# Attention beside a spectral filter on one core: four zero matmuls left out, and the last matmuls of seven units moved behind scores

## The chip, the core and the metric

The kernel runs on one core of a Trainium2 chip. The metric is the device time of one execution in microseconds. The kernel before took 424.93 us in the median of three runs (424.67 to 424.96).

## What is computed

From x of 2048 x 448 the kernel computes a gated sum of two results. `a` is softmax attention with 16 heads of 28 columns each, `b` is a two-dimensional real Fourier transform, a product with given complex weights, and the inverse transform. The reference, cut to that:

```python
x = A_x
g = sigmoid((x * gate_w).sum(-1, keepdims=True))

qkv = (x @ wqkv).reshape(B, S, 3, H, Dh).transpose(2, 0, 3, 1, 4)
q, k, v = qkv[0], qkv[1], qkv[2]
scores = jnp.einsum("bhqd,bhkd->bhqk", q, k) * Dh ** -0.5
o = jnp.einsum("bhqk,bhkd->bhqd", softmax(scores, axis=-1), v)
a = o.transpose(0, 2, 1, 3).reshape(B, S, D) @ wo

X = rfft2(x.astype(float32), axes=(-2, -1)) * (w_r + 1j * w_i)
b = irfft2(X, s=(S, D), axes=(-2, -1)).astype(bfloat16)

out = g * a + (1 - g) * b
```

B is 1, S is 2048, D is 448, H is 16 and Dh is 28; the inputs are bfloat16.

## The kernel before

**Blocks of scores.** The scores of a head are 2048 x 2048. They are cut into blocks of 128 keys by 512 queries. A block is one matmul that uses 32 rows of the TensorE array (`score`, L834). Four heads make a group T (0 to 3), and a group has four blocks of queries, so c runs over 16 blocks of (group, queries); each has 16 blocks of keys, i, and four heads.

**Two ways to an exponential.** Most blocks go to ScalarE: two or three of them are written to a tile in PSUM (`ps2` or `ps3`, in turn), and one exp of 1024 or 1536 columns reads the tile (`exp`, L1092). Other blocks are packed for VectorE: `away` (L1054) writes one score block to a background bank, VectorE turns it into 16-bit integers (L850), and when four are together a chain of VectorE steps makes the exponential out of them (L870, L873, L878, L882, L885, L896 and L904, or a transfer that adds, L899, in place of the last). The chain's steps wait in a list, `vq`, and are put out one by one with `fill_v` or `hurry`.

**Values.** `do_pv` (L1440) multiplies the finished exponentials with the values: four matmuls of 32 columns of the array for each block of keys (L1013), summed in the PSUM bank `psPV`.

**Units.** All other work is cut into units, which share two PSUM banks called `bg0` and `bg1` with the packed scores. A unit has phases; a phase is some matmuls (`pe`) and what empties the bank again (`ve`), with planned costs. Of those that the change names:
- `V5`, `V9` and `V15` are value projections (`v_unit`, L500): four matmuls of 336 columns (L506) into one bank, each adding the next part of the inner dimension, and one cast (L510) that takes the sum out. Unit Vt gives the values of key block t.
- `q1.3`, `k2.1`, `q3.0` and `q3.2` are projections of q or k (`qk_unit`, L554; the first digit is the group, the second the block of 512 columns): four matmuls of 512 columns (L290, in `project`) and one cast (L562).

Other units that stand beside them: parts of the transforms (L678 and L683; L699 to L721 for the column transforms, of which L746 to L758 are the second kind of inputs; L771 to L791 for the inverse), each with its bank and its eviction.

**The order.** The order of instructions on every engine is worked out while the kernel is built. `stream` (L1368) runs one iteration k for each exp: it emits exp k, then values (`do_pv`), then units (`pick` chooses one, `step` at L1240 emits its next phase), then zero matmuls, then the scores for exp k+2 (`scores`, L1016). The planner keeps a clock for each engine: `self.tp` for TensorE, `self.tv` for VectorE, `self.ta` for ScalarE. It moves them by constants written in the code, and asks by them whether a phase still fits. `self.bank_free` holds when a bank should be empty, and a new unit takes the bank that is free first. The engines themselves wait for each other's results by semaphores, in the planned order.

**Behind scores.** A phase named in the set `BEHIND` (L56) is planned at its place in the iteration, but its matmuls and its eviction go to a list, `self.behind`, that is run right after `scores` in the same iteration. A packed score whose eviction comes up while that list is not empty puts it in the list as well (`pack_step`).

**Zero matmuls.** TensorE gets matmuls of zeros where it would otherwise have too little to do. `dummy` calls `one_zero` until the last iterations and this one have enough columns; `until` calls it where it would wait. `one_zero` (L1332) adds a matmul of zeros to `psPV` (L1334), or writes one to a free bank by `zero` (L1328). Each is 512 columns of the whole array. `zeros` (L1049) writes one of 32 rows beside the scores where no packed score goes there.

Of the kernel before, what the change touches and what calls it, by code (L numbers as in the profile page):

```python
# [25 lines left out]
NT = 16  # L26
# [6 lines left out]
NC = 16  # L33
# [10 lines left out]
E_SC, E_EX, E_PV, E_PV2, E_MM = 0.32, 0.05, 0.33, 0.215, 0.22  # L44
# [9 lines left out]
LATER = 70.0  # L54

BEHIND = {("T2.0", 1), ("T2.2", 1), ("q0.2", 1), ("f1.5", 1), ("I.0", 1), ("I.6", 1), ("base14", 3), ("out4", 3), ("out6", 2)}  # L56
NPT = 4
NPD = 5
CLAIM, LAST = 10, 8
# [25 lines left out]
def with_free(ap, free):  # L85

    return _AP(tensor=ap.tensor, offset=ap.offset, ap=[list(ap.ap[0])] + [list(x) for x in free])
# [77 lines left out]
class Kernel:  # L165
# [19 lines left out]
    def setup(self):  # L185
# [5 lines left out]
        self.rot5 = ctx.enter_context(tc.tile_pool(name="rot5", bufs=5))  # L191
        self.pts = ctx.enter_context(tc.tile_pool(name="pts", bufs=NPT))
        self.pd = ctx.enter_context(tc.tile_pool(name="pd", bufs=NPD))
# [306 lines left out]
    def v_unit(self, t):  # L500

        nc = self.nc

        def pe(ps):
            for c in range(4):
                nc.tensor.matmul(ps[:, 0:D - DC], lhsT=self.xT[:, c, 128 * t:128 * t + 128],  # L506
                                 rhs=self.Wqkv[:, c, 2 * D + DC:3 * D], start=(c == 0), stop=(c == 3))

        def ve(ps):
            nc.vector.tensor_copy(out=self.vsb[:, t, 4:H, 0:DH],  # L510
                                  in_=ps[:, 0:D - DC].rearrange("p (h d) -> p h d", d=DH))
        return Unit(f"V{t}", [(pe, 0.68, 1344, ve, 0.42)], needs=["W3"])
# [41 lines left out]
    def qk_unit(self, T, q, b):  # L554
        nc = self.nc

        def pe(ps):
            self.project(ps, T, q, b)

        def ve(ps):  # L560
            dst = (self.kT if q else self.qT)[T][:, 512 * b:512 * b + 512]
            nc.vector.tensor_copy(out=dst, in_=ps[:])  # L562
            if b == 3:
                self.vq.insert(0, (squares, E_TT, None))

        def squares():
            sq = self.marks[f"sq{T}{q}"] = self.rot1.tile([P, S], BF16, name="sq")
            src = (self.kT if q else self.qT)[T][:]
            nc.vector.tensor_tensor(out=sq[:], in0=src, in1=src, op=ALU.mult)
            self.marks[f"sqt{T}{q}"] = self.tv + 0.1  # L570
        needs = [f"{'qk'[q]}{T}.{b - 1}"] if b else [f"Wg{T}"] if q else [f"kn{T}"]
        return Unit(f"{'qk'[q]}{T}.{b}", [(pe, 0.96, 2048, ve, 0.60)], needs=needs)
# [509 lines left out]
    def exp(self, k):  # L1082
# [5 lines left out]
        early = self.early[k % 2]  # L1088
        assert k // 2 < len(early) + NPT or k - 2 * NPT not in live, (k, live)
        w = 2 if k % 2 else 3  # L1090
# [149 lines left out]
    def step(self, u, b, limit):  # L1240

        pe, cost, cols, ve, vcost = u.phases[0]
        start = max(self.tp, self.bank_free[b])
        if start + cost > limit:
            return False
        if b not in self.open:
            self.take(u)
            self.open[b] = u, self.bank(b)
            self.begun |= u.name == "W0"
        self.until(start)  # L1250
        ps = self.open[b][1]
        n = len(self.vq)
        self.hurry()
        self.fill_v(start + cost + PV - 0.3)
        self.fewer = len(self.vq) < n
        more = 0.0
        if (u.name, len(u.phases)) in BEHIND:

            self.behind.append(lambda: pe(ps))
            if ve is not None:  # L1260
                self.behind.append(lambda ve=ve: ve(ps))
                ve = self.later
            more = 1.0 if u.name == "T2.0" else 0.0
        else:
            pe(ps)
        self.tp = start + cost
        self.add(self.tp, cols)
        u.phases.pop(0)
        if ve is not None:
            self.dve(vcost, at=self.tp + PV)  # L1270
            if u.name == "T3.0" and any(x.name == "k0.1" for x, _ in self.open.values()):

                self.held = lambda: ve(ps)
            else:
                ve(ps)
            self.bank_free[b] = self.tv + VP + more
            if u.name == "k0.1" and not u.phases and self.held:
                self.held()
                self.held = None
                self.bank_free[0:2] = self.bank_free[1] + 0.6, self.bank_free[0]  # L1280
        if not u.phases:
            del self.open[b]
            if b == 2:
                self.psPV = self.bank(2)
                self.pv_free = self.bank_free[2]
            self.marks[u.name] = max(self.tv, self.tp) + u.lag
        return True
# [42 lines left out]
        self.dummies += 1  # L1330

    def one_zero(self):  # L1332
        if self.pv_open and not self.ended:
            self.nc.tensor.matmul(self.psPV[:], lhsT=self.warm[:], rhs=with_free(self.warm[:], [[0, 4], [1, P]]), start=False, stop=False,  # L1334
                                  skip_group_check=True)
            self.add(self.tp + E_MM, 512)
            self.dummies += 1
        elif not self.ended and self.pv_c < NC and 2 not in self.open and self.tp >= self.pv_free:
            self.zero(self.psPV, self.tp)
        else:  # L1340
            b = [i for i in (0, 1) if self.bank_free[i] <= self.tp and i not in self.open]
            if not b:
                return False
            self.zero(self.psp.tile([P, 512], F32, name=f"bg{b[0]}", tag=f"bg{b[0]}", bufs=1), self.tp)
        return True
# [22 lines left out]
    def stream(self):  # L1368
# [4 lines left out]
        self.dummies = self.owed = 0  # L1373
        self.ended, self.ot, self.held, self.next_exp = False, None, None, None
        self.behind = []
        self.pv_c, self.pv_free, self.pv_open = 0, 0.0, False
        for n in (3, 2):
            self.psp.tile([P, n, QW], F32, name=f"ps{n}", tag=f"ps{n}", bufs=1)
# [6 lines left out]
        b = self.per.tile([P, 3, QW], BF16, name="early3", tag="Bd_inv")  # L1385
# [9 lines left out]
        k = -1  # L1395
        more = False
        while self.ring:
            k += 1
            if "T3.2" in self.marks and not more:

                more = True
                e = self.per.tile([P, 14, QW], BF16, name="early2", tag="xtok_UT")
                self.early[0].extend(e[:, 3 * j:3 * j + 3] for j in range(2))
                self.early[1].extend(e[:, 6 + 2 * j:8 + 2 * j] for j in range(4))
            self.exp(k)
            size = len(self.tiles[k])
            self.ta = end = max(self.ta, self.sc[k] + E_TAIL) + E_EXP[size]
            nxt = len(self.tiles[k + 1]) if self.ring else 3
            limit = end + E_EXP[nxt] - 0.50 - E_TAIL
            self.tp = max(self.tp, end - E_EXP[size] - 0.2)  # L1410
            self.groups()
            self.do_pv(k, left, 4 if not self.free[NC - 1] else 3 if self.tp < 2 * BEGIN else 2, end + AP)
            while True:
                self.run_events()
                if not self.ring:

                    self.do_pv(k, left, NT)
                    break
                u = self.pick()
                if u is None and self.tp < BEGIN:  # L1420

                    t = self.ready()
                    if self.tp < t < limit:
                        self.until(t)
                        continue
                if u is None or not self.step(*u, limit):
                    break
            if self.ring:
                self.dummy()
            if self.act_c < NC:  # L1430
                self.until(end + AP)
            self.scores(k + 2, end)
            while self.behind:
                self.behind.pop(0)()
            self.fill_v(end - 0.2)
            self.log.append((k, end, self.tp, self.tv, len(self.vq), len(self.mand), self.dummies,
                             self.live, len([p for p in self.pieces if self.pack_t.get(p)]), self.pv_c))
# [222 lines left out]
```

## Time and profile before

| | |
|---|---|
| median of three runs | 424.93 us (424.67 to 424.96) |
| the profiled execution's own time | 424.69 us |
| its span, first to last instruction | 422.9 us |
| granted TensorE clock, mean | 1.000 |
| instructions | 8345 |
| exps, L1092 | 358, of which 339 into `Pt` |
| score matmuls, L834 | 926 to `ps`, 130 to `bg` |
| values matmuls from the tiles, L1013 | 818 |
| zero matmuls into `psPV`, L1334 | 124 |
| zero matmuls beside scores, L1049 | 91 |
| q, k casts, L562 | 24, 0.68 us each |
| V casts, L510 | 16, 0.50 us each |

The profile is of one execution. PE is TensorE's matmuls and PEld its weight loads, DVE is VectorE, ACT is ScalarE, POOL is GpSimd, SP is the engine that issues most transfers. L12 is line 12 of the kernel.

The page gives the busy time of each engine with its share of the span, and then the costliest groups of instructions. A row of a group has the line, the engine, the operation, what it writes and reads with the tile's shape, the count, the busy time in us with the mean of one in ns, and the idle time of the engine just before them, with what ended most of it.

A timeline lists groups in order of time, with the start in us from the span's start, how long the group took, the engine, the line, the operation, the tiles, the count, and in brackets idle time of the engine ahead of it with what ended it. A score matmul has the form `32*128` there, a values matmul `128*32`, a projection or a zero `128*128`: rows and columns of the array that it uses.

### The profile page before, as it was taken

Reading aid. Unit: us, or ns where it says so; the run is one execution under the profiler, and the core shown is the slowest. Engines: PE = TensorE matmul, PEld = TensorE weight load, DVE = VectorE, ACT = ScalarE, POOL = GpSimd, SP = SyncE. Lnnn points to the kernel's source line nnn. Section 1 sums busy time; section 2 is a strip of 40 time slices with the busy share of each in tenths; the row PEclk is TensorE's granted clock in tenths of the full one; section 3 lists DMA queues with packets and bytes.
Section 4 is the critical chain, followed back from the end, with each engine's and each line's share of the span. In section 5 each row is a group of like instructions: output and inputs, shape, how many; then the busy total and the mean of one; then the engine's idle time right before and its main releaser. Section 6 shows DMA issues by size and latency. Waiting matters only on the chain.

```text
span 422.9 us, 8345 instructions
## 1 busy us (share of the span) xinstructions
PE 406.7 (96%) x3196; PEld 144.5 (34%) x3196; DVE 392.6 (93%) x651; ACT 411.5 (97%) x369; POOL 61.3 (14%) x95
## 2 busy tenths in 40 slices
PE   8999999999999999999999999999999999999995
PEld 4343233333333333333333333333344332332232
DVE  6669989999899999999999999999999999999995
ACT  4999999999999999999999999999999999999994
POOL 6000002030100112012220100202002021310000
PEclk9999999999999999999999999999999999999999
DMA  9900301331302152375664446536553304233032
GB/s 234 180 8 2 8 27 31 90 72 32 76 15 47 24 101 59 73 169 103 153 154 96 105 103 117 112 71 109 111 146 81 77 2 91 49 76 78 22 74 67
DMA packets 32404, 34.30 MB, mean 81 GB/s; under 512 B 14988, under 2 KB 25228, under 8 KB 32332
## 3 DMA queue, kind: packets, MB, share of 16 engines
q1 hardware_dynamic: 28012, 20.21, 20.8%
q0 software_dynamic: 3600, 13.11, 17.1%
q8 instruction: 25, 0.41, 0.4%
q10 hardware_dynamic: 752, 0.44, 0.3%
q14 instruction: 15, 0.12, 0.1%
HBM read 14.85 MB, written 1.95 MB: 40 GB/s over the span
## 4 chain that ended last, share of the span: by engine, by line
PE 37%; ACT 30%; DVE 17%; issue 8%; DMA 6%; SPq 1%; DVEq 0%; ACTq 0%
ACT Pt L1092 28%; PE psPV L1013 7%; PE ps L834 6%; PE bg L834 4%; PE psPV L1334 4%; DVE Pd L850 4%; PE bg L290 3%; PE bg L1049 2%; DMA Fc<-cF 2%; DMA Wo<-in_A_wo_dram 2%; DVE pa L896 2%; ACT early L1092 2%; PE bg L678 1%; DVE U L689 1%; PE bg L506 1%
## 5 line engine op out<-in xcount | busy, mean ns | idle before, releaser
L1092 ACT ACTIVATE Pt<-ps 128x1024 bf16<-128x1024 f32 (+1 forms) x339 | 385.6, 1301 | 0.6 <-PE ps L834 0.2
L834 PE MATMUL ps<-qT,kT 32*128 32x512 bf16 (+2 forms) x926 | 143.3, 375 | 3.3 <-ACT Pt L1092 2.0
L850 DVE TENSOR_SCALAR Pd<-bg 128x512 uint16<-128x512 f32 x130 | 88.7, 683 | 5.0 <-PE ps L834 3.6
L1013 PE MATMUL psPV<-Pt,vsb 128*32 128x512 bf16 x818 | 79.9, 388 | 0.0
L834 PEld LDWEIGHTS <-kT 32*128 32x128 bf16 x1056 | 45.3, 91 | 93.7 <-issue 88.2
L899 POOL DMA_DIRECT2D Pd<-pa x25 | 23.7, 950 | 207.6 <-PE ps L834 89.0
L834 PE MATMUL bg<-qT,kT 32*128 32x512 bf16 x130 | 49.8, 383 | 1.2 <-DVE nM L651 0.4
L986 POOL TENSOR_TENSOR oT<-o,rep 128x128 bf16<-128x128 f32 x52 | 28.4, 572 | 132.3 <-DVE oT L983 73.2
L896 DVE TENSOR_TENSOR pa<-pa,n 128x2048 uint16<-128x2048 f16 (+2 forms) x33 | 40.1, 1214 | 0.6
L1013 PEld LDWEIGHTS <-vsb 128*32 128x32 bf16 x1008 | 23.1, 93 | 50.6 <-issue 50.0
L882 DVE TENSOR_TENSOR pa<-pa,n 128x2048 f16<-128x2048 f16 (+1 forms) x33 | 40.0, 1211 | 0.3
L1334 PE MATMUL psPV<-warm 128*128 128x512 bf16 x124 | 40.1, 385 | 0.0
L1049 PE MATMUL bg<-warm 32*128 32x512 bf16 x91 | 34.9, 383 | 1.4 <-DVE Pd L850 1.2
L290 PE MATMUL bg<-xT,Wg 128*128 128x512 bf16 (+1 forms) x112 | 29.6, 381 | 0.2
L873 DVE TENSOR_SCALAR Pd<-Pd 128x2048 uint16<-128x2048 uint16 (+1 forms) x33 | 23.2, 703 | 0.4
L870 DVE TENSOR_SCALAR n<-Pd 128x2048 uint16<-128x2048 uint16 (+1 forms) x33 | 22.5, 682 | 0.5
L689 DVE CAST U<-bg 128x450 bf16<-128x450 f32 x32 | 19.9, 622 | 3.1 <-PE bg L721 1.3
L885 DVE TENSOR_SCALAR pa<-pa 128x2048 f16<-128x2048 f16 (+1 forms) x33 | 22.5, 681 | 0.1
L878 DVE TENSOR_SCALAR pa<-n 128x2048 f16<-128x2048 uint16 (+1 forms) x33 | 22.3, 675 | 0.0
L1049 PEld LDWEIGHTS <-warm 32*128 32x128 bf16 x91 | 8.2, 90 | 29.0 <-issue 27.9
L787 PE MATMUL bg<-Binv,VT 128*128 128x448 bf16 x64 | 16.9, 355 | 0.2
L1092 ACT ACTIVATE early<-ps 128x1024 bf16<-128x1024 f32 (+1 forms) x13 | 15.3, 1264 | 1.0 <-PE ps L834 1.0
(189 smaller groups left out, 429.0 us busy)
## 6 DMA issues: line engine op xcount, KB each, us to landing
Pd<-pa POOLq DMA_DIRECT2D x25, 512.0 KB, 5.0
rep<-rD SPq DMA_DIRECT2D x52, 64.0 KB
CR<-cRB SPq DMA_DIRECT2D x8, 256.0 KB
UT<-U SPq DMA_DIRECT2D x16, 112.5 KB
VT<-U SPq DMA_DIRECT2D x16, 112.5 KB
CR<-cCS SPq DMA_DIRECT2D x8, 192.0 KB
xtok<-in_A_x_dram SPq DMA_DIRECT2D x3, 448.0 KB
out_dram<-fin SPq DMA_DIRECT2D x12, 112.0 KB
```

The costliest lines, as they stand in the source:

```text
L290: self.nc.tensor.matmul(ps[:], lhsT=self.Wg[T, q][0:k, c, :], rhs=self.xT[0:k, c, 512 * b:512 * b + 512], start=(c == 0), stop=(c == 3))
L689: self.nc.vector.tensor_copy(out=U[:], in_=ps[:, 0:F2])
L834: self.nc.tensor.matmul(out[:, w * j:w * j + w], lhsT=self.kT[T][32 * h:32 * h + 32, 128 * i:128 * i + 128], rhs=self.qT[T][32 * h:32 * h ...
L850: nc.vector.tensor_scalar(out=pk["t"][:, h, :], in0=ps[:], scalar1=SCALE * LOG2E * 512.0, scalar2=127.0 * 512.0, op0=ALU.mult, op1=ALU.add)
L882: v.tensor_tensor(out=st["a"], in0=st["a"], in1=st["n"], op=ALU.mult)
L896: v.tensor_tensor(out=q, in0=st["a"], in1=st["n"], op=ALU.mult)
L899: nc.gpsimd.dma_start(out=t, in_=q, accum_op=ALU.add)
L986: nc.gpsimd.tensor_tensor(out=o[:, e:e + P], in0=o32[:, e:e + P], in1=st["rep"][:, e:e + P], op=ALU.mult)
L1013: self.nc.tensor.matmul(self.psPV[32 * h:32 * h + 32, :], lhsT=self.vsb[:, i, 4 * T + h, :], rhs=pcs[h], start=first, stop=last, tile_posi ...
L1049: self.nc.tensor.matmul(ps[:], lhsT=self.warm[sl], rhs=with_free(self.warm[sl], [[0, 4], [1, P]]), start=True, stop=True, tile_position=(3 ...
L1092: self.nc.scalar.activation(out=Pt[:, 0:n, :], in_=ps[:, 0:n, :], func=ACT.Exp, scale=SCALE)
L1334: self.nc.tensor.matmul(self.psPV[:], lhsT=self.warm[:], rhs=with_free(self.warm[:], [[0, 4], [1, P]]), start=False, stop=False, skip_grou ...
```

## The change

`SPARED` names four iterations, 13, 116, 156 and 304, with one zero matmul each. In these iterations the first call of `one_zero` keeps its place in the planner's accounts (columns and count) but issues nothing. `ENDS` names seven units with how many of their four matmuls are moved: one for V5, V9, V15, q1.3, k2.1 and q3.0, and two for q3.2. `step` emits the others at the unit's place, and puts the last one or two, and the cast that empties the bank, on the list that runs behind the iteration's scores. The planner's clocks and the time at which it takes the bank to be empty are the same as before.

Put beside the old order, TensorE has four matmuls and four weight loads less and eight matmuls at a later place. VectorE's order differs in one place: at q3.0 a chain step (L870) that stood behind the cast now stands ahead of it. ScalarE, GpSimd and SP have the same order.

The diff is whole:

```diff
--- before.py
+++ after.py
@@ -54,6 +54,10 @@
 LATER = 70.0
 
 BEHIND = {("T2.0", 1), ("T2.2", 1), ("q0.2", 1), ("f1.5", 1), ("I.0", 1), ("I.6", 1), ("base14", 3), ("out4", 3), ("out6", 2)}
+
+SPARED = {13: 1, 116: 1, 156: 1, 304: 1}
+
+ENDS = {"V5": 1, "V9": 1, "V15": 1, "q1.3": 1, "k2.1": 1, "q3.0": 1, "q3.2": 2}
 NPT = 4
 NPD = 5
 CLAIM, LAST = 10, 8
@@ -501,8 +505,8 @@
 
         nc = self.nc
 
-        def pe(ps):
-            for c in range(4):
+        def pe(ps, part=range(4)):
+            for c in part:
                 nc.tensor.matmul(ps[:, 0:D - DC], lhsT=self.xT[:, c, 128 * t:128 * t + 128],
                                  rhs=self.Wqkv[:, c, 2 * D + DC:3 * D], start=(c == 0), stop=(c == 3))
 
@@ -554,8 +558,8 @@
     def qk_unit(self, T, q, b):
         nc = self.nc
 
-        def pe(ps):
-            self.project(ps, T, q, b)
+        def pe(ps, part=range(4)):
+            self.project(ps, T, q, b, True, part)
 
         def ve(ps):
             dst = (self.kT if q else self.qT)[T][:, 512 * b:512 * b + 512]
@@ -1261,6 +1265,12 @@
                 self.behind.append(lambda ve=ve: ve(ps))
                 ve = self.later
             more = 1.0 if u.name == "T2.0" else 0.0
+        elif u.name in ENDS:
+            n = 4 - ENDS[u.name]
+            pe(ps, range(n))
+            self.behind.append(lambda: pe(ps, range(n, 4)))
+            self.behind.append(lambda ve=ve: ve(ps))
+            ve = self.later
         else:
             pe(ps)
         self.tp = start + cost
@@ -1330,7 +1340,11 @@
         self.dummies += 1
 
     def one_zero(self):
-        if self.pv_open and not self.ended:
+        if self.spare[self.k]:
+            self.spare[self.k] -= 1
+            self.add(self.tp + E_MM, 512)
+            self.dummies += 1
+        elif self.pv_open and not self.ended:
             self.nc.tensor.matmul(self.psPV[:], lhsT=self.warm[:], rhs=with_free(self.warm[:], [[0, 4], [1, P]]), start=False, stop=False,
                                   skip_group_check=True)
             self.add(self.tp + E_MM, 512)
@@ -1373,6 +1387,7 @@
         self.dummies = self.owed = 0
         self.ended, self.ot, self.held, self.next_exp = False, None, None, None
         self.behind = []
+        self.spare = dict.fromkeys(range(-1, 4 * NC * NT), 0) | SPARED
         self.pv_c, self.pv_free, self.pv_open = 0, 0.0, False
         for n in (3, 2):
             self.psp.tile([P, n, QW], F32, name=f"ps{n}", tag=f"ps{n}", bufs=1)
@@ -1402,6 +1417,7 @@
                 e = self.per.tile([P, 14, QW], BF16, name="early2", tag="xtok_UT")
                 self.early[0].extend(e[:, 3 * j:3 * j + 3] for j in range(2))
                 self.early[1].extend(e[:, 6 + 2 * j:8 + 2 * j] for j in range(4))
+            self.k = k
             self.exp(k)
             size = len(self.tiles[k])
             self.ta = end = max(self.ta, self.sc[k] + E_TAIL) + E_EXP[size]
```

## The prediction

> **What bounds the kernel now.** I read the page's shares first, then the costliest groups, then the trace in order of time around each edited place.
>
> ```profile
> PE 406.7 (96%) x3196; PEld 144.5 (34%) x3196; DVE 392.6 (93%) x651; ACT 411.5 (97%) x369; POOL 61.3 (14%) x95
> ...
> L1092 ACT ACTIVATE Pt<-ps 128x1024 bf16<-128x1024 f32 (+1 forms) x339 | 385.6, 1301 | 0.6 <-PE ps L834 0.2
> L834 PE MATMUL ps<-qT,kT 32*128 32x512 bf16 (+2 forms) x926 | 143.3, 375 | 3.3 <-ACT Pt L1092 2.0
> ```
>
> Three engines are over 90% busy, and ScalarE (ACT) runs one exp after the other. From start to start, the trace has 1.33 us behind an exp of three score blocks and 0.90 behind one of two; whatever is longer is a stall. I number the exps 0 to 357. Before those that the change aims at, ACT stands: exp 60 for 0.17 us, 75 0.20, 78 0.18, 88 0.18, 99 0.22, 118 0.17, 158 0.14, 208 0.23, 222 0.39, 306 0.23; and exp 15 0.15. A stall of ACT is paid in full unless a later one shrinks for it. But an exp gained is only kept if TensorE (PE) and VectorE (DVE) also bring the next scores sooner. So I follow each edit for the tiles behind it.
>
> The rules of spacing come from the same rows: 512-wide matmuls of one shape start 0.216 us apart, 336-wide ones 0.143; between shapes (128 rows, 32 rows for scores, 32 columns for values) the step is 0.31 to 0.32, or 0.24 behind a 336-wide one; scores start 0.05 after the exp that reads their tile ends; an exp starts 0.10 to 0.14 after its scores end; an eviction on DVE starts 0.04 after its matmul ends, and the next matmul in that bank 0.05 after the eviction.
>
> Here is q3.2, which loses two matmuls, then V5's eviction and what DVE does behind it, then one place of zeros.
>
> ```profile
> 260.86 0.68 DVE L850 TENSOR_SCALAR Pd<-bg 128x512 uint16<-128x512 f32 x1
> ...
> 261.00 1.02 PE L290 MATMUL bg<-xT,Wg 128*128 128x512 bf16 x4
> ...
> 261.95 0.38 PE L834 MATMUL bg<-qT,kT 32*128 32x512 bf16 x1
> 261.96 0.59 PE L834 MATMUL ps<-qT,kT 32*128 32x512 bf16 x3
> 262.06 0.69 DVE L562 CAST qT<-bg 128x512 bf16<-128x512 f32 x1
> ...
> 262.67 2.37 ACT L1092 ACTIVATE Pt<-ps 128x1536 bf16<-128x1536 f32 x2 [0.23 <-PE ps L834]
> ...
> 262.82 0.36 PE L746 MATMUL bg<-UT,CR 128*128 128x450 bf16 x1
> ...
> 263.31 0.39 PE L834 MATMUL ps<-qT,kT 32*128 32x512 bf16 x2
> ```
>
> ```profile
> 76.82 0.68 DVE L873 TENSOR_SCALAR Pd<-Pd 128x2048 uint16<-128x2048 uint16 x1
> 77.42 0.50 DVE L510 CAST vsb<-bg 128x336 bf16<-128x336 f32 x1
> 77.84 0.68 DVE L850 TENSOR_SCALAR Pd<-bg 128x512 uint16<-128x512 f32 x1
> 78.44 0.68 DVE L878 TENSOR_SCALAR pa<-n 128x2048 f16<-128x2048 uint16 x1
> 79.15 1.23 DVE L882 TENSOR_TENSOR pa<-pa,n 128x2048 f16<-128x2048 f16 x1
> 80.30 0.68 DVE L562 CAST qT<-bg 128x512 bf16<-128x512 f32 x1
> ```
>
> ```profile
> 142.81 0.81 PE L1328 MATMUL psPV<-warm 128*128 128x512 bf16 x3
> ...
> 143.55 0.39 PE L834 MATMUL ps<-qT,kT 32*128 32x512 bf16 x3
> ```
>
> In the first the reader sees four matmuls of q3.2, the scores behind them, the exp that stood 0.23 us idle for them, and L746, the next unit, which takes the very bank that L562 empties. In the second DVE has no idle time in brackets: it is the bound of that stretch. In the third, three zeros stand between PE and the scores.
>
> **The change part by part.** Put beside the old order, the new order of instructions drops four matmuls with their weight loads, moves eight, and changes one place on DVE; ACT, GpSimd and SP keep theirs, so no transfer moves in its queue.
>
> *Zeros*, 0.216 us each. Iteration 13: exp 15 stood for the small activation L491 (26.41 to 26.56); its scores had been done for 0.25 us: 0. Iteration 116: exp 116 ends at 143.11, so the scores may start from 143.16, and come at 143.33 in place of 143.55; exp 118 gains its whole 0.17 and the next one's stall shrinks too: -0.20. Iteration 156: exp 156 ends at 188.71, so the scores (188.82) gain 0.06, and exp 160, which waits for a full PE (stall 0.11), takes it back: 0. Iteration 304: exp 304 ends at 356.93, the scores are at 357.03: 0.05, which the PE-bound stalls near 370 take back. Sum -0.20; from -0.54 (every stall gone) to 0.
>
> *q3.2.* The pack's score in front of the three needs its bank, freed by L850 at 261.54: scores from 261.59 (were 261.95), exp 222 at 262.31, -0.36. The pair then starts at 262.13 and 262.35 and ends at 262.73; L562 runs 262.77 to 263.46 instead of 262.06 to 262.75. L746 waits for it: 263.51 (was 262.82). The scores behind it come at 264.00 (263.31), end at 264.39, and exp 223 starts at 264.49 where it had 264.01: +0.48. Queued behind L562 on DVE is the pack's L850, which L712 waits for, equally late; so nothing catches up. Bounds -0.36 to +0.69 (the whole lateness). I take +0.48.
>
> *q3.0.* The same picture: scores 245.91 to 245.70, exp 208 -0.22; the last matmul 246.02, ends 246.40; L562 at 246.44 (was 246.02); the next L746, again in its bank, at 247.18 (was 246.76); exp 209 +0.36. The one step that DVE does earlier, L870, fills the 0.53 us in which DVE stood here anyway. +0.36, bounds -0.22 to +0.42.
>
> *V5.* Scores 77.23 to 77.09, exp 60 -0.14. Its last matmul starts at 77.41 and ends at 77.71: L510 at 77.75, +0.33. DVE is full, so the L562 at 80.30 is as late; V7's first matmul (81.03) waits for that bank and becomes 81.36, its scores 82.03, and exp 64, which had 0.05 to spare, comes +0.28. Bounds -0.14 to +0.33.
>
> *V9.* The pack's bank is freed by L562 (93.64 to 94.32) and scores are at 94.43: only -0.06. PE pays two shape changes more, 0.07 net, and exp 78, which waits for values matmuls (next item), is +0.07. DVE is 0.20 late besides. +0.07, bounds -0.06 to +0.20.
>
> *q1.3.* Exp 78 doesn't wait for its scores (done at 97.86) but for values matmuls that read its buffer: they start at 97.80, end at 98.19, and it starts at 98.29. With the last matmul between, they start at 98.01 (scores from 97.37, held by exp 76; matmul 97.69): +0.21, bounds -0.10 to +0.38 (DVE's lateness).
>
> *V15.* Scores and exp 88 -0.14. DVE is in L882 until 109.82, so L510 isn't late; but PE is 0.10 longer, and exp 90 stands right at PE: 0, bounds -0.14 to +0.10.
>
> *k2.1.* Scores 121.78 to 121.56, but exp 99 started 0.38 us behind their end, for something that I can't name: 0, from -0.22 to +0.10 at that place. L562 goes from 122.01 to 122.30, DVE is full behind it, k2.2's matmuls wait for the L850 at 123.21, and exp 103 comes +0.28. Bounds -0.22 to +0.28.
>
> Sum: -0.20 + 0.48 + 0.36 + 0.28 + 0.07 + 0.21 + 0 + 0.28 = +1.48 us. The profiled execution took 424.69 (span 422.9 and 1.8 around it), 0.24 under the median 424.93 and within the runs' spread of 0.29. From it the sum is 426.2, from the median 426.4; I give 426.3.
>
> A step between array shapes costs 0.31 to 0.32 in the rows against 0.216 without one, and a moved matmul adds one such step, 0.10 us. The Trainium skill, in TensorEngine Tiling (Array Packing), section Tiling Modes, Key Properties, says "Changing tiling mode (not just tile) drains the TensorE", which speaks against parking a full-array matmul between scores and values; the rows agree. If PE's own length decided, as that rule reads, the time would be the third rival's.
>
> **The rivals.** *All stalls go*, and whatever comes late is absorbed: 0.14 + 0.06 + 0.10 + 0.14 + 0.22 + 0.22 + 0.36 at the units, 0.17 + 0.06 + 0.05 at the zeros, 1.52 us: 423.4. For it: these are among the largest stalls of the stream. Against it: L746 stood right behind L562 (0.07 us) in the same bank.
> *DVE's lateness is absorbed* where the next user of the bank is units away: V5 -0.14, V9 -0.06, V15 -0.14, k2.1 0, with q1.3 +0.21, q3.0 +0.36, q3.2 +0.48 and zeros -0.20: +0.5, 425.4. Against it: DVE's rows without a gap.
> *PE's length decides*: 4 x 0.216 = 0.86 less, 7 x 0.10 = 0.70 more, -0.16: 424.8. For it 96% busy; against it that PE still waits for ACT (2.0 us in the group above).
> *The clock drops* where zeros are gone. The first matmuls of the program took 603 ns where later ones take 384; one stretch of 15 matmuls so slowed, each 0.22 longer, costs 3.3 us: 428.2. Against it: in the five stretches of 3 to 4 us that I asked for around the edits PE is 82% to 100% busy and the granted clock 1.00 in each, so 0.6 us of standing in 3.4 cost no clock, and a zero is 0.216. It would decide once PE stands for longer than that.
>
> **How the numbers follow.** Forecast 0.67, its own range 425.7 to 427.2 (the DVE items halved; q3.2 and q3.0 at their ends). All stalls go 0.10, DVE absorbed 0.15, PE's length 0.06, clock 0.02. Changes under 0.2%, 0.85 us, can't be told from none here: slower 0.69, same 0.21, faster 0.10. The range runs from the third rival less the runs' spread, 424.5, to the forecast's upper end plus about as much, 427.4; it leaves out the first rival, the last, and some 0.05 of the forecast.
>
> **What would show it.** Exp 222 about 0.36 earlier against exp 221, and exp 223 about 0.8 later against 222; PE idle before q3.2's following L746 (line 750 then), released by the cast that was L562; V5's L510 starting 0.04 behind its last matmul with DVE idle ahead of it; exp 118 without a stall. I am wrong if PE's rows behind the moved matmuls start when they did, or if DVE shows idle time between V5's eviction and V7's.

## The result, and the profile after

| | before | changed |
|---|---|---|
| median of 7 runs each, us | 424.85 (424.66 to 425.18) | 426.19 (426.01 to 426.73) |
| the profiled execution's span, us | 422.9 | 424.2 |
| granted TensorE clock, mean | 1.000 | 1.000 |
| instructions | 8345 | 8337 |

The ratio is 1.0029 with a 95% interval of 1.0020 to 1.0039; by the medians the change costs 1.34 us. Differences below are of medians too; the ratios beside them are over the single executions, and in the last three experiments where two of the 27 executions of before took 428.92 and 429.72 us, they lie about 0.001 below the ratio of the medians. The changed kernel's line numbers are 4 higher than before from L57 on, and 10 to 16 higher from L1264 on: the cast L562 is L566, the cast L510 is L514, the score L834 is L838, the exp L1092 is L1096, the next unit's L746 is L750.

The costliest groups of the changed kernel, in the order of the page and then of the list of groups; the last column is the engine's idle time ahead of the group, and what ended it:

```profile
PE 407.2 (96%) x3192; PEld 144.9 (34%) x3192; DVE 393.2 (93%) x651; ACT 411.4 (97%) x369; POOL 61.5 (14%) x95
...
L1096 ACT ACTIVATE Pt<-ps 128x1024 bf16<-128x1024 f32 (+1 forms) x339 | 385.6, 1314 | 1.9 <-PE ps L838 1.2
```

```profile
L566 DVE CAST qT<-bg 128x512 bf16<-128x512 f32 x12 | 8.2, 685 | 1.1 <-PE bg L294 1.0
...
L750 PE MATMUL bg<-UT,CR 128*128 128x450 bf16 x16 | 5.8, 361 | 1.0 <-DVE qT L566 0.9
```

The same two groups in the kernel before:

```profile
L562 DVE CAST qT<-bg 128x512 bf16<-128x512 f32 x12 | 8.2, 684 | 0.5 <-PE bg L290 0.5
...
L746 PE MATMUL bg<-UT,CR 128*128 128x450 bf16 x16 | 5.8, 361 | 0.2
```

ScalarE does the same work in the same time (385.6 us), and stands 1.9 us ahead of its exps where it stood 0.6: these 1.3 us are the loss. The first matmul of a transform unit, L750, now waits 0.9 us in all for the cast of a moved q unit, where the same group had 0.2 us of idle time and no such releaser. The casts of q themselves wait 1.0 us for their matmuls, where they waited 0.5.

That is one picture, seen at q3.0 and at q3.2: the last matmul late, the cast late, the next unit's matmul late, the exp late. Here it is at q3.2, in order of time:

```profile
261.71 0.59 PE L294 MATMUL bg<-xT,Wg 128*128 128x512 bf16 x2
...
262.31 0.37 PE L838 MATMUL bg<-qT,kT 32*128 32x512 bf16 x1
...
262.47 0.43 PE L838 MATMUL ps<-qT,kT 32*128 32x512 bf16 x3
...
262.83 0.60 PE L294 MATMUL bg<-xT,Wg 128*128 128x512 bf16 x2
...
263.47 0.69 DVE L566 CAST qT<-bg 128x512 bf16<-128x512 f32 x1 [0.61 <-PE bg L294]
...
264.21 0.35 PE L750 MATMUL bg<-UT,CR 128*128 128x450 bf16 x1 [0.45 <-DVE qT L566]
...
264.69 0.39 PE L838 MATMUL ps<-qT,kT 32*128 32x512 bf16 x2
...
265.18 2.37 ACT L1096 ACTIVATE Pt<-ps 128x1024 bf16<-128x1024 f32 x2 [0.51 <-PE ps L838]
```

The scores stand behind two matmuls instead of four, and exp 222 lost its stall. But VectorE stood 0.61 us idle until the moved pair was done, PE 0.45 until the cast was done, and ScalarE 0.51 until the scores behind L750 were. Exp 223 starts 2.08 us behind exp 222, where it started 1.35 behind.

To see where time came and went I put the start of each of the 358 exps beside its start in the trace of before. The difference changes in a few places only. The table has its steps, and what is kept of them where the next edit's first step comes (the 0.04 us by which the first exp starts later is taken off):

| edit | steps of the exps' lateness, us | kept, us | forecast |
|---|---|---|---|
| V5 | exp 60 -0.17, exp 64 +0.51 | +0.35 | +0.28 |
| V9 and q1.3 | exp 75 -0.10, exp 78 +0.28 | +0.19 | +0.28 |
| V15 | exp 88 -0.17, exp 90 +0.20 | +0.05 | 0 |
| k2.1 | exp 99 -0.22, exps 102 and 103 +0.45 | +0.17 | +0.28 |
| zero of 116 | exp 118 -0.17 | -0.19 | -0.20 |
| zero of 156 | exp 158 -0.14, 160 -0.06, 177 +0.08 | -0.12 | 0 |
| q3.0 | exp 208 -0.23, exp 209 +0.60, 210 +0.07, 215 -0.08 | +0.34 | +0.36 |
| q3.2 | exp 222 -0.39, exp 223 +0.73, 227 +0.18, 232 -0.09 | +0.48 | +0.48 |
| zero of 304 | exp 306 -0.23, exp 317 +0.15 | 0.00 | 0 |
| sum | | +1.27 | +1.48 |

Steps under 0.05 us are in the third column alone; the largest is -0.05 at exp 108, which the table counts to k2.1.

### The profile page after: what moved, and what is told of

It is laid out like the page before. It is cut to its first block, busy times and chain, and to the rows that moved or that the text cites. A ratio compares the mean times of both kernels' runs of the same rounds, so it can differ in the third digit from the quotient of the medians.

```text
span 424.2 us, 8337 instructions
## 1 busy us (share of the span) xinstructions
PE 407.2 (96%) x3192; PEld 144.9 (34%) x3192; DVE 393.2 (93%) x651; ACT 411.4 (97%) x369; POOL 61.5 (14%) x95
## 4 chain that ended last, share of the span: by engine, by line
PE 43%; ACT 30%; DVE 15%; issue 7%; DMA 4%; SPq 1%; POOL 0%; DVEq 0%; ACTq 0%; POOLq 0%
ACT Pt L1096 26%; PE psPV L1017 8%; PE ps L838 7%; PE bg L838 5%; PE psPV L1348 4%; PE bg L294 4%; PE bg L1053 3%; DVE Pd L854 3%; PE bg L510 2%; ACT early L1096 2%; PE bg L682 2%; DMA Wv<-in_gate_w_dram 2%; DVE pa L900 2%; DVE U L693 1%; DVE pa L886 1%
## 5 line engine op out<-in xcount | busy, mean ns | idle before, releaser
L1096 ACT ACTIVATE Pt<-ps 128x1024 bf16<-128x1024 f32 (+1 forms) x339 | 385.6, 1314 | 1.9 <-PE ps L838 1.2
L838 PE MATMUL ps<-qT,kT 32*128 32x512 bf16 (+2 forms) x926 | 142.6, 375 | 3.6 <-ACT Pt L1096 2.0
L854 DVE TENSOR_SCALAR Pd<-bg 128x512 uint16<-128x512 f32 x130 | 88.7, 682 | 4.7 <-PE ps L838 3.0
L838 PEld LDWEIGHTS <-kT 32*128 32x128 bf16 x1056 | 45.8, 91 | 94.5 <-issue 89.2
L903 POOL DMA_DIRECT2D Pd<-pa x25 | 24.6, 982 | 208.9 <-PE ps L838 88.0
L838 PE MATMUL bg<-qT,kT 32*128 32x512 bf16 x130 | 49.8, 383 | 1.1 <-DVE nM L655 0.3
L1096 ACT ACTIVATE early<-ps 128x1024 bf16<-128x1024 f32 (+1 forms) x13 | 15.3, 1264 | 1.0 <-PE ps L838 1.0
```

The costliest lines, as they stand in the source:

```text
L838: self.nc.tensor.matmul(out[:, w * j:w * j + w], lhsT=self.kT[T][32 * h:32 * h + 32, 128 * i:128 * i + 128], rhs=self.qT[T][32 * h:32 * h ...
L854: nc.vector.tensor_scalar(out=pk["t"][:, h, :], in0=ps[:], scalar1=SCALE * LOG2E * 512.0, scalar2=127.0 * 512.0, op0=ALU.mult, op1=ALU.add)
L903: nc.gpsimd.dma_start(out=t, in_=q, accum_op=ALU.add)
L1096: self.nc.scalar.activation(out=Pt[:, 0:n, :], in_=ps[:, 0:n, :], func=ACT.Exp, scale=SCALE)
```

## Experiments

All times of before in this section are of the same chip as the kernel beside them: 424.99 us in the median, over 21 and then 27 runs.

**Zeros alone and moves alone.** First the four zeros without the moves (`ENDS = {}`).

> The four zeros left out, no unit touched. My theory: exp 118 starts 0.17 us earlier than in the kernel before, exp 158 0.14 and exp 306 0.23 earlier against the exps ahead of them (as in the trace of after), and a part comes back near exps 177 and 317, so the end is 0.2 to 0.45 us earlier: 424.4 to 424.65 beside 424.85. Rival, zeros and moves help each other: less than 0.1 us here. Rival, the clock: a granted clock under 1.00 and a time above that of before.

Measured: 424.81 us (ratio 0.9996, 0.9987 to 1.0004), -0.18 us. That is just under the 0.2 to 0.45 us that were expected. In the trace exp 118 starts 0.17 earlier, 158 0.14 and 306 0.23 against the exps ahead of them, as expected to the hundredth, and at exp 160 0.40 us is won. By exp 177 it is all given back in this execution, and at exp 174 the reason is no zero. VectorE's own line in order of time:

```profile
201.59 0.25 DVE L965 RECIPROCAL i<-r 128x16 f32<-128x16 f32 x1 [0.44 <-DMA r<-o]
```

A transfer of sums that this step needs landed 0.44 us after VectorE had come to it. Behind that, a transform unit's first matmul (L750, at 206.49) stands 0.34 us for an eviction on VectorE, and the scores of exp 174 stand behind it. The traces of before and of the changed kernel show no wait at that transfer. So the zeros brought the steps that were expected of them; what of it reaches the end also depended on a transfer in this execution (its last exp is 0.11 late, though the median is 0.18 us less), and the 0.18 us can't be told from nothing.

Then all moves with the four zeros kept (`SPARED = {}`).

> All four zeros kept, all seven units' ends moved. If zeros and moves add up: the changed kernel's 1.34 us plus the 0.2 to 0.45 that the zeros gave, so 1.55 to 1.8 above before. Rival, they don't add (moved matmuls stand where zeros were missing): 1.34 or less.

Measured: 426.56 us (ratio 1.0039, 1.0027 to 1.0052), 1.57 us more; by the exps, 1.61 more. Moves and zeros add up within the noise: 1.57 - 0.18 is 1.39, and the changed kernel has 1.34. The steps at the moved units agree with those of the changed kernel to 0.02 us in all (exp 64 +0.50, 209 +0.60, 223 +0.73), so neither is an accident of one execution.

**Three moves alone.** V5, q3.0 and q3.2 have the largest steps in the table.

```diff
-SPARED = {13: 1, 116: 1, 156: 1, 304: 1}
+SPARED = {}
-ENDS = {"V5": 1, "V9": 1, "V15": 1, "q1.3": 1, "k2.1": 1, "q3.0": 1, "q3.2": 2}
+ENDS = {"V5": 1, "q3.0": 1, "q3.2": 2}
```

> Only V5, q3.0 and q3.2 moved, no zero left out. By the trace of after: V5 -0.17 then +0.50 at exp 64, q3.0 -0.23 then +0.60 at exp 209, q3.2 -0.39 then +0.73 at exp 223 and some 0.1 behind it; together 1.1 to 1.3 us above before. If these losses came from the other moves around them: under 0.6.

Measured: 426.23 us (ratio 1.0032, 1.0019 to 1.0045), 1.24 us more, and 1.23 by the exps. These three make 1.24 of the 1.57 us that all seven moves cost.

**The same three moves, and the bank taken out of the way.** In each of these iterations a packed score stands ahead of the scores, in the other bank, and its eviction goes out behind the unit's cast. Here it goes out ahead of the cast, into the time in which VectorE stood idle, and the planner's two bank times are exchanged, so that the next unit takes the bank that is emptied first. PE's order stays that of three_moved.

```diff
 ENDS = {"V5": 1, "q3.0": 1, "q3.2": 2}
+FIRST_OUT = {"V5", "q3.0", "q3.2"}
+OTHER = {"V5", "q3.0", "q3.2"}
...
-        self.behind.append(ve) if self.behind else ve()
+        if self.pack_out is not None:
+            ve()
+            self.pack_out = True
+        else:
+            self.behind.append(ve) if self.behind else ve()
...
             pe(ps, range(n))
+            self.pack_out = False if u.name in FIRST_OUT else None
+            self.other = u.name in OTHER
...
                 self.behind.pop(0)()
+            if self.pack_out and self.other:
+                self.bank_free[0], self.bank_free[1] = self.bank_free[1], self.bank_free[0]
+            self.pack_out = None
```

> The same three units moved, but the packed score's eviction of that iteration goes out on VectorE before the unit's cast, and the unit that follows takes the packed score's bank. Theory of the bank: the next unit no longer waits for the late cast, so exps 60, 208 and 222 keep their gain (-0.14 to -0.39) and exps 64, 209 and 223 lose only 0.15 to 0.35 in place of 0.50 to 0.73; in all 0.3 us above before (0 to 0.5). Rival, the moved matmuls cost by themselves, by their shape steps and by the values that they hold up: as three_moved, 1.1 to 1.3.

Measured: 425.13 us (ratio 1.0001, 0.9992 to 1.0010), 0.14 more than before and 1.10 less than three_moved. Exps 60, 208 and 222 keep their gains (-0.14, -0.21, -0.39); exps 64, 209 and 223 lose 0.22, 0.25 and 0.23, and exp 227 loses 0.28, where it lost 0.17 in three_moved. The same stretch at q3.2 (line numbers are 4 to 8 higher than in the changed kernel: L858 is the packed score's eviction, L570 the cast, L754 the next unit):

```profile
261.66 0.37 PE L842 MATMUL bg<-qT,kT 32*128 32x512 bf16 x1 [0.22 <-DVE Pd L858]
...
262.12 0.68 DVE L858 TENSOR_SCALAR Pd<-bg 128x512 uint16<-128x512 f32 x1
262.18 0.60 PE L298 MATMUL bg<-xT,Wg 128*128 128x512 bf16 x2
...
262.82 0.69 DVE L570 CAST qT<-bg 128x512 bf16<-128x512 f32 x1
263.04 0.36 PE L754 MATMUL bg<-UT,CR 128*128 128x450 bf16 x1
```

The cast still starts 0.04 us behind the moved pair's end. VectorE has no idle time ahead of it any more, and L754 starts while the cast runs, without a wait: it has the bank that L858 emptied. Moved matmuls, their shape steps and the values that they hold up are all still there; what is gone is the wait for the cast.

**The same eviction order, the old bank.** Two things changed at once there, so the exchange of banks is now left out (`OTHER = set()`).

> As three_other_bank, with the packed score's eviction ahead of the unit's cast on VectorE, but the next unit stays in the moved unit's bank. Theory of the bank: the cast is as late as before, so the next unit waits for it as in three_moved: 1.1 to 1.5 us above before, exps 64, 209 and 223 late by 0.4 to 0.9 again. Rival, VectorE's order alone made three_other_bank fast: 0.0 to 0.4.

Measured: 426.37 us (ratio 1.0023, 1.0002 to 1.0044), 1.38 more. Exp 209 loses 0.85 and exp 223 loses 0.74. Exp 64 loses only 0.08, below the 0.4 to 0.9 expected, but exp 62 loses 0.29 ahead of it. At q3.0:

```profile
246.58 0.69 DVE L858 TENSOR_SCALAR Pd<-bg 128x512 uint16<-128x512 f32 x1
...
247.19 0.68 DVE L570 CAST qT<-bg 128x512 bf16<-128x512 f32 x1
247.92 0.35 PE L754 MATMUL bg<-UT,CR 128*128 128x450 bf16 x1 [0.72 <-DVE qT L570]
...
248.89 2.46 ACT L1104 ACTIVATE Pt<-ps 128x1024 bf16<-128x1024 f32 x2 [0.75 <-PE ps L842]
```

L754 stands 0.72 us for the cast, and ScalarE 0.75 for the scores behind it. At q3.0 and q3.2 VectorE's order alone helps nothing; the bank decides. At V5 the order is worth something. There the cast (L518 here) is later still, and the unit behind V5, which has its bank, stands for it:

```profile
78.90 1.02 PE L298 MATMUL bg<-xT,Wg 128*128 128x512 bf16 x3 [0.29 <-DVE vsb L518]
```

But VectorE does not stand idle ahead of that cast, and V7's first matmul (L514, at 81.51) waits for nothing, where it stood 0.39 us for VectorE in three_moved. The exps keep 0.26 us of lateness behind V5, for 0.36 in three_moved and 0.11 in three_other_bank. The exchange of banks without the new order on VectorE was not run.

**q1.3 behind the values.** For q1.3 the forecast named another wait: exp 78 waits for values matmuls that read the buffer it writes. If so, putting the moved matmul behind those values as well must take that wait away, and make the cast's worse.

```diff
-            self.behind.append(lambda: pe(ps, range(n, 4)))
-            self.behind.append(lambda ve=ve: ve(ps))
+            self.past.append(lambda: pe(ps, range(n, 4)))
+            self.past.append(lambda ve=ve: ve(ps))
...
             self.do_pv(k, left, 4 if not self.free[NC - 1] else 3 if self.tp < 2 * BEGIN else 2, end + AP)
+            while self.past:
+                self.past.pop(0)()
```

> Only q1.3's last matmul and its cast moved, and these not behind the scores but behind the next values too; no zero left out. My theory of q1.3: exp 78 waits for the values matmuls that read its buffer, not for its scores, so it is no longer 0.28 late but 0.05 to 0.10 early; the cast is later still, so exp 79 loses 0.35 to 0.5, and in all it is 0.5 to 0.9 us above before. Rival, exp 78 waits for something else behind the moved matmul: exp 78 late by about 0.28 as in the changed kernel.

Measured: 425.41 us, 0.42 more by the medians; the ratio, 0.9995 (0.9968 to 1.0023), can't tell it from before. The trace can: exp 78 is 0.10 early, exp 79 0.48 late, and 0.50 is left at the end. In order of time:

```profile
97.70 0.61 PE L1017 MATMUL psPV<-Pt,vsb 128*32 128x512 bf16 x8
98.25 0.39 PE L294 MATMUL bg<-xT,Wg 128*128 128x512 bf16 x1
...
98.67 0.69 DVE L566 CAST qT<-bg 128x512 bf16<-128x512 f32 x1 [0.86 <-PE bg L294]
...
99.42 0.37 PE L838 MATMUL bg<-qT,kT 32*128 32x512 bf16 x1 [0.21 <-DVE qT L566]
```

The values start at 97.70, and exp 78 no longer stands for them. In the changed kernel they started at 98.37, where the exps were 0.39 us late already, and exp 78 stood for them:

```profile
98.87 1.45 ACT L1096 ACTIVATE Pt<-ps 128x1536 bf16<-128x1536 f32 x1 [0.32 <-PE psPV L1017]
```

With the last matmul past the values, the cast starts 0.86 us later than VectorE could have, and the packed score that follows waits for it.

**A version without moves.** The zeros that gained and the moves that lost suggest leaving out more zeros and moving nothing. I took iterations in which a zero stands between PE and scores for which ScalarE has to wait.

```diff
-SPARED = {13: 1, 116: 1, 156: 1, 304: 1}
+SPARED = {28: 1, 29: 1, 75: 1, 116: 1, 156: 1, 178: 1, 304: 1}
-ENDS = {"V5": 1, "V9": 1, "V15": 1, "q1.3": 1, "k2.1": 1, "q3.0": 1, "q3.2": 2}
+ENDS = {}
```

> No unit touched; one zero each left out in iterations 28, 29, 75, 116, 156, 178 and 304, where zeros stand between TensorE and scores that ScalarE waits for. If each stall that a zero makes is gained: exps 30 to 32 0.14 to 0.20 earlier, 78 0.10, 118 0.17, 158 0.14, 180 0.08, 306 0.23, of which 0.1 to 0.3 comes back: 0.5 to 0.8 us under before. Rival, the gain is lost again to waits that have nothing to do with zeros, as at exp 174 in zeros_only: 0 to 0.25 under before.

Measured: 424.34 us (ratio 0.9974, 0.9953 to 0.9994), 0.65 less than before. The steps came as expected: exp 30 -0.14, 78 -0.10, 118 -0.17, 158 -0.14, 180 -0.08, 306 -0.23; 0.11 comes back at exp 177 and 0.15 at exp 317; 0.56 is left at the end. Its median is below that of both kernels, by a small amount and with an interval that nearly reaches 1.

## Why the prediction was right, step by step

The forecast was 426.3, and 426.19 was measured; +1.48 us was the sum and +1.34 the difference of the medians. By the exps the parts make +1.27. V5 cost 0.07 more than its term and V15 0.05 more; V9 with q1.3 came 0.09 under, k2.1 0.11, q3.0 0.02, and iteration 156 gave 0.12 that the sum did not have. These errors cancel in part, so some of the closeness is luck. The two signs by which the forecast would have been wrong did not show: the rows of PE behind the moved matmuls start later, and VectorE has no idle time between the evictions of V5 and V7 (77.80 to 82.30).

*q3.2 and q3.0* came out as worked out: exp 222 0.36 earlier (0.39 measured), exp 223 then 0.84 later against it (0.73), +0.48 kept (+0.48); q3.0 +0.36 kept (+0.34). At q3.2 the mechanism was right and the last hundredths were luck: at exp 223 only 0.34 was lost in all, and the rest came at exp 227, which stood 0.13 us for values matmuls, a wait that the sum did not have. The reason given, that L746 stands in the moved unit's bank, was shown by the pair of runs: with the other bank most of the loss goes, with VectorE's order alone none of it.

*V5*: the cast was to be 0.33 late and nothing to catch up behind it on VectorE. In the changed kernel the cast starts 0.04 behind its last matmul's end, with 0.26 us of idle VectorE ahead, and V7's first matmul waits 0.38 us for the L566 that is late because of it:

```profile
77.80 0.51 DVE L514 CAST vsb<-bg 128x336 bf16<-128x336 f32 x1 [0.26 <-PE bg L510]
...
80.69 0.68 DVE L566 CAST qT<-bg 128x512 bf16<-128x512 f32 x1
...
81.42 0.73 PE L510 MATMUL bg<-Wqkv,xT 128*128 128x336 bf16 x4 [0.38 <-DVE qT L566]
...
82.62 1.45 ACT L1096 ACTIVATE Pt<-ps 128x1536 bf16<-128x1536 f32 x1 [0.22 <-PE ps L838]
```

The sum had +0.28, the trace +0.35. The lateness went through 3.6 us of VectorE's work and two units without becoming less.

*V9 and q1.3*: +0.28 together, +0.19 measured. The mechanism of q1.3 stands (exp 78 waits for the values, as the trace says and the experiment shows). The values' start, 98.37 less the 0.39 us by which the exps were late already, is 0.18 later than in the kernel before, where the sum had 0.21 for q1.3 and 0.07 for V9 on top. So the two do not add at this exp; V9 was not moved alone.

*V15* 0, +0.05 measured: the gain of 0.17 goes back at exp 90 because PE is longer there. Around it the moved matmul starts 0.33 us behind the scores and the values 0.24 behind that, where the values stood 0.32 behind the scores; with the 0.14 that it leaves at its old place that is 0.11, and the sum had 0.10.

*k2.1*: the sum gave exp 99 nothing, since it started 0.38 behind its scores for a reason that I could not name. In the changed kernel it started 0.22 earlier, 1.33 behind exp 98, which is ScalarE's own spacing; what it had waited for before stays open. The way back was the forecast's: k2.2's first matmul, at 124.86, stood 0.35 us for the eviction L854. But 0.45 came back at exps 102 and 103, less 0.05 at exp 108, for 0.28 in the sum. Kept is +0.17 for +0.28; the gain that was not foreseen and the larger loss partly cancel, which is luck.

*Zeros*: iteration 116 as worked out. For 156 and 304 the term was too small: the sum took the gain from the start of the scores, 0.06 and 0.05. In the trace the exps gained 0.14 and 0.23. The reason is the packed score ahead of the three. For 304, first in the kernel before and then in the changed one:

```profile
357.03 0.38 PE L834 MATMUL bg<-qT,kT 32*128 32x512 bf16 x1
357.04 0.59 PE L834 MATMUL ps<-qT,kT 32*128 32x512 bf16 x3
```

```profile
358.02 0.39 PE L838 MATMUL bg<-qT,kT 32*128 32x512 bf16 x1
...
358.29 0.39 PE L838 MATMUL ps<-qT,kT 32*128 32x512 bf16 x3
```

The packed score and the first of the three started together before, and the three took 0.59 us; now the packed score is 0.27 ahead, and the three take 0.39 (why it matters here is said in the last section). The exp waits for the last of them, so 0.20 more is gained than their start shows. For 304 the gain came back (0.15 of it at exp 317), as the sum had it. For 156 the sum had exp 160 take the gain back, and it gained 0.06 more; 0.08 came back at exp 177, and 0.12 was kept as far as q3.0, the largest error of the sum. zeros_only shows that such a gain can be lost to a transfer.

*The rivals.* Nine of the stalls went or shrank, 1.8 us of the exps' time, so "all stalls go" was right in its first half; 3.1 us of lateness came behind them. VectorE's lateness was not absorbed: V5 lost 0.51 us at exp 64 and k2.1 0.45 at exps 102 and 103, where that rival lost nothing. PE's length decides at V15, where it cost 0.05, and not at the end. The granted clock is 1.000 in the mean of the profiled execution, as before.

The Trainium skill's sentence, in TensorEngine Tiling (Array Packing), section Tiling Modes, Key Properties, that changing the tiling mode drains the TensorE was weighed as a reason against the moves. The step that goes with it, about 0.1 us for each moved matmul, is in the trace (V15 above); three_other_bank, with the same steps on PE and 0.14 us of loss for 1.24, shows that it was not the main part of what the change cost.

## What to carry to other kernels

Before a matmul is moved past others, ask who empties its bank and who fills it next: moving the last matmul of a sum moves the eviction, and with it the next tenant's first matmul, and on a full VectorE everything that is queued behind the eviction. If the move is wanted, the plan has to know the bank's new time, so that the next unit goes where an eviction is done, and another eviction has to fill the time in which VectorE would stand idle for the late one; here the two together were worth 1.10 us of 1.24. A stall that is 0.2 to 0.4 us long is gained only as far as nothing else is due right behind it, so follow one edit for at least two or three tiles before it is given a value.

## What the runs showed that I had not expected

The steps in the exps' lateness are the same from execution to execution to about 0.01 us (exp 223 +0.729 in the changed kernel, in moves_only and in three_moved; exp 209 +0.602 in all three), though the times of whole runs of one kernel spread by 0.5 us and more. Edits of this size could be read from one trace where times needed many runs. That holds where no transfer comes in between: in zeros_only one trace shows 0.35 us at exp 174 that no other kernel's trace has.

Three score matmuls take 0.39 us from the first's start to the last's end, or 0.6, by the packed score that starts with them. A score uses the 32 rows of its head (`tile_position=(32 * h, 0)` in `score`), and the packed score's head is by the planned order sometimes one of the three heads beside it. In the kernel before, a packed score starts at most 0.05 us ahead of three scores 37 times. In 30 of them its rows are those of none of the three, and the three take 0.39 to 0.40 us; V5's is one:

```profile
77.23 0.38 PE L834 MATMUL bg<-qT,kT 32*128 32x512 bf16 x1
77.23 0.39 PE L834 MATMUL ps<-qT,kT 32*128 32x512 bf16 x3
```

In the other 7 it has the rows of one of the three, and they take 0.56 to 0.60 us; iterations 156 and 304 and that of q3.2 are among these. So at iteration 304 a score 0.27 us out of the way was worth 0.20 at the other end, and at V5 it could not have been.
